# Reordering the head of a fused attention and feed-forward kernel: K/V products pair by pair, input weights in row blocks of 512 columns, hidden units in fours

## The chip, the cores and the metric

The kernel runs on one core of a Trainium2 chip. The time is the device time of one execution in microseconds (us); lower is better. Most executions of one kernel here lie within about 1 us of each other, and much of this study is about differences of 0.3 to 1.5 us in 286, so every version was timed in several rounds beside the kernel before, and each profile, which is one single execution, is used for what happens inside it and not for its total.

A ratio below is the mean time of one kernel's fast runs over that of the other's fast runs of the same rounds, so it is not quite the ratio of the medians that stand beside it.

## The reference

Eight batches of linear attention (softmax of q over the 64 features, softmax of k over the 576 rows, so that K and V shrink to a 64x64 matrix per head), followed by a feed-forward block with 2048 hidden units and a Swish with one beta per unit.

```python
q_s = softmax(q, axis=-1)                       # q, k, v: (8, 8, 576, 64) f32
k_s = softmax(k, axis=2)
kv  = einsum('bhsd,bhse->bhde', k_s, v)
x   = einsum('bhsd,bhde->bhse', q_s, kv)        # then reshaped to (4608, 512)
h   = x @ w_in                                  # (512, 2048)
g   = h * (1 / (1 + exp(-beta * h)))
out = g @ w_out                                 # (2048, 512), out f32
```

## The kernel before

TensorE multiplies in bf16. The tokens are cut in nine slabs of 512. A slab has a first phase (`pass1`: 16 tiles of 128 hidden units, each the sum of four matmuls over the input pairs m = 0 to 3) and a second phase (`pass2`: 64 matmuls into four output tiles). The K/V products and attention outputs of the next batch are woven between the matmuls of the slab before. Slab 0 has nothing before it, so its attention (the *head*) is bare, and batch 1's attention is squeezed into the end of slab 0 (the *transition*) because its data land late (a load of V for batch 1 at 40.0 us by the chain of the kernel before).

Names in the code and the profiles: EK holds the exponentials of k and VB the values in bf16, whose products are the K/V products; KVD is a K/V product after normalisation, QT the transposed softmax of q, XT the attention output, which is the input of the first phase; WIN and WOUT are the two weight matrices in bf16 (w_out divided by beta), GT the hidden units after the Swish, PS a bank of PSUM, which every matmul on the pages has as its output.

The parts that matter (cuts are marked with `...`):

```python
WCH = ((0, 256), (256, 256), (512, 512), (1024, 512), (1536, 512))   # chunks of w_in columns

def pass1_mm(t, f, m, bk):
    ...
    n = 2 if f < 8 else 4            # hidden units of tile f: every n-th column
    l = bass.AP(WIN, m * DFF + 128 * (f // n * n) + f % n, [[NM * DFF, 128], [n, 128]])
    mm(PS[bk][:, :], l, x[:, m, :], m == 0, m == NM - 1, ...)

def homes_ek(i, e_, r=()):           # zero the unused blocks of EK; r only says when
    z = EK[i][64 * e_:64 * e_ + 64, :, :, 64 * (1 - e_):64 * (2 - e_)]
    add(POOL, lambda e: e.memset(z.bitcast(F32), 0.0), r=r, w=[("ekz", i, e_)])

# head: K/V products of all pairs, then the outputs; pairs 2 and 3 in halves
kv_mm(0, 0, 3, 0); kv_mm(0, 1, 3, 1)
for hp in range(2): kvd(0, hp, 3, VW * hp)          # VectorE: normalise into KVD
kv_mm(0, 2, 5, 0, D + 1); out_now(0, 0, 4, ACTE)
kv_mm(0, 3, 5, 1, D + 1); out_now(0, 1, 6, ACTE)
...
at(0); out_halves(0, 2, 7, 3); out_halves(0, 3, 4, 5)   # only two tiles of slab 0 by m
...
for c in range(2, len(WCH)):
    for m in range(NM): cast_win(c, m, 1, DVE)      # f32 -> bf16 on VectorE
for e_ in range(2):
    homes_ek(1, e_, [("win", 3, NM - 1)])           # after the casts of columns 1024 to 1535
for c in range(3): load_wout(c)
load_main("qf", qt_h, QF, 1, 4); load_wout(3)
...
# slab 1: small products of the 64 remainder rows of batches 0 and 1
todo = spread(outr_steps(1), 101.5, 103) + attn_late(2)
```

The second number in `todo` is a position counted in matmuls of the slab: 64 is the first matmul of the second phase. QTR, which `outr_steps` reads, is filled by a transposing DMA.

The softmax here doesn't subtract the row's maximum and nothing guards it: scores larger than these inputs give would overflow.

Of the kernel before, what the change touches and what calls it, by code (L numbers as in the profile page):

```python
# [8 lines left out]
ALU = mybir.AluOpType  # L9
# [19 lines left out]
FG = {2: (0, 256, 512, 768), 4: (1024, 1536)}  # L29
WCH = ((0, 256), (256, 256), (512, 512), (1024, 512), (1536, 512))  # L30
# [128 lines left out]
def bass_efficient_attn_shen__then__act_swish_beta_kernel(  # L159
# [12 lines left out]
    with ExitStack() as es:  # L172
# [363 lines left out]
        def out_halves(b, hp, *bks):  # L536
            i = b % 2
            for e_, (eng, key, bk) in enumerate(((DVE, "xt", bks[0]), (ACTE, "xh", bks[1]))):
                c = slice(256 * e_, 256 * e_ + 256)
                mm(PS[bk][:, c], KVD[i][:, hp, :], QT[i][:, hp, c], True, True,  # L540
                   r=kvk(i, hp) + [("qt", i, hp)], w=[("ps", bk)], bk=bk)
                add(eng, lambda e, eng=eng, bk=bk, c=c: (e.copy if eng == ACTE else e.tensor_copy)(
                    XT[i][:, hp, c], PS[bk][:, c]),
                    r=[("ps", bk)], w=[(key, i, hp)], bank=[bk])

        def go(steps):
            for s in steps:
# [6 lines left out]
        SKEY = ([("wst", 0, 0), ("wst", 0, 1), ("wst", 2)], [("wst", 1), ("wst", 3)], [("o2", 1, u) for u in range(4)],  # L554
                [("o2", 0, u) for u in range(4)])

        def load_wout(c):
            n = 2 if c < 2 else 4
            a = bass.AP(wout_h, 512 * c * DM, [[n * DM, 128], [128 * n * DM, 4 // n], [1, n * DM]])
            o = bass.AP(STAGE[c], 0, [[4 * DM, 128], [n * DM, 4 // n], [1, n * DM]])  # L560
            add(SP, lambda e: e.dma_start(o, a), w=SKEY[c],  # L561
                slot=f"wst{c}")

        def scale_wout(c):
            for f in range(4 * c, 4 * c + 4):
                add(DVE, lambda e, f=f: e.tensor_scalar(
                    WOUT[:, f, :], STAGE[c][:, f % 4, :], RB[:, f:f + 1], None, ALU.mult),
                    r=SKEY[c] + ["rb"], w=[("wout", f)])


        HEAD = (1, 2, 3, 4, 5, 6, 7)

        def wkeys(c, m, nm):
            if c == 0:
                return [("wst", 0, h) for h in range(m // 2, (m + nm + 1) // 2)]
            if c == 2:
                return SKEY[1][m // 2:(m + nm + 1) // 2]
            return SKEY[0][2:] if c == 1 else SKEY[c - 1]

        def load_win(c, m=0, nm=NM):  # L580
            c0, n = WCH[c]
            a = bass.AP(win_h, m * 128 * DFF + c0, [[DFF, 128], [128 * DFF, nm], [1, n]])
            s = STAGE[c0 // 512][:, m:m + nm, c0 % 512:c0 % 512 + n]
            add(SP, lambda e: e.dma_start(s, a), w=wkeys(c, m, nm), slot=f"win{c}{m}")  # L584

        def cast_win(c, m, nm, eng):
            c0, n = WCH[c]
            x = m if nm == 1 else slice(m, m + nm)
            s = STAGE[c0 // 512][:, x, c0 % 512:c0 % 512 + n]
            add(eng, lambda e: e.tensor_copy(WIN[:, x, c0:c0 + n], s), r=wkeys(c, m, nm),  # L590
                w=[("win", c, y) for y in range(m, m + nm)])

        def turn_beta():
            bb, c0 = kb, 16
            for g, n, o in ((4, 4, 0), (2, 2, 0), (2, 2, 256)):
                for k_ in range(n):
                    mm(bass.AP(PS[bb], c0 + o // 128 + k_, [[512, 128], [4, g]]),
                       bass.AP(BT, o + k_, [[512, g], [n, 128]]), IDF[0:g, 0:g],
                       True, True, r=["bt", "idf"], w=[("ps", bb)], bk=bb, tr=True)

        def read_beta():
            bb, c0 = kb, 16
            pb = PS[bb][:, c0:c0 + NF]
            add(DVE, lambda e: e.tensor_scalar(BC[:, :], pb, -1e-20, None,
                                               ALU.is_gt),
                r=[("ps", bb)], w=["bc0"], bank=[bb])
            yield
            add(DVE, lambda e: e.scalar_tensor_tensor(BC[:, :], pb, 1e-20, BC[:, :],
                                                      ALU.is_lt, ALU.mult),
                r=[("ps", bb), "bc0"], w=["bc"], bank=[bb])  # L610
            add(DVE, lambda e: e.scalar_tensor_tensor(BETA[:, :], BC[:, :], 4e-20,
                                                      pb, ALU.mult, ALU.add),
                r=["bc", ("ps", bb)], w=["beta"], bank=[bb])
            yield
            add(DVE, lambda e: e.reciprocal(RB[:, :], BETA[:, :]), r=["beta"], w=["rb"])
            yield
# [5 lines left out]
        kb = bank(HEAD)  # L622
        warm(3, 0, True)
        exp_q(0)
        exp_kh(0, 0, 1, 0)
        exp_kh(0, 0, 1, 1)
        exp_kh(0, 1, 1, 1)
        exp_kh(0, 1, 1, 0)
# [4 lines left out]
        go(t_steps(0, (0,), HEAD))  # L633
# [4 lines left out]
        go(t_steps(0, (1,), HEAD))  # L638
        warm(1, 0, True)
        for c in range(len(WCH)):  # L640
            for m in (0, 2) if c in (0, 2) else (0,):
                load_win(c, m, 2 if c in (0, 2) else NM)
        cast_v(0, 0)
        cast_v(0, 2)
        cast_v(0, 3, POOL, 1)
        for m in range(NM):
            cast_win(0, m, 1, POOL)
        cast_win(1, 0, 2, POOL)
        go(t_steps(0, (2,), HEAD))
        warm(1, 0, True)  # L650
        cast_v(0, 1, DVE)
        go(t_steps(0, (3,), (1,)))
        ksum(0, 0, kb)
        ksum(0, 1, kb)
        ksum_inv(0, kb, 0, 2, 0, 1)
        cast_v(0, 3, ACTE, 0)
# [3 lines left out]
        def pass1_mm(t, f, m, bk):  # L660
            x = XT8 if t == 8 else XT[t % 2]
            rd = [("xt8", p_) for p_ in range(4)] if t == 8 else [("xt", t % 2, m)]
            if (t, m) in ((0, 2), (0, 3), (1, 2), (1, 3)):
                rd = rd + [("xh", t, m)]
            n = 2 if f < 8 else 4
            l = bass.AP(WIN, m * DFF + 128 * (f // n * n) + f % n, [[NM * DFF, 128], [n, 128]])
            mm(PS[bk][:, :], l, x[:, m, :], m == 0, m == NM - 1,
               r=rd + [("win", c, m) for c in range(len(WCH))
                       if WCH[c][0] <= 128 * (f // n * n) < WCH[c][0] + WCH[c][1]],
               w=[("ps", bk)], bk=bk)  # L670
# [5 lines left out]
        HFIRST = ((0, 1, 2, 4, 6, 7, 0, 1, 2, 7), (0, 2, 4, 1, 3, 6, 5, 7, 4))  # L676
# [4 lines left out]
        def first_tiles(t, n):  # L681
            bks = [hbank(t, k) for k in range(n)]

            def at(m, f0=0, f1=n):
                for f in range(f0, f1):
                    pass1_mm(t, f, m, bks[f])
            return at
# [7 lines left out]
        FIRST = (2, 5)  # L695
        TT = (107, 125)
        at = first_tiles(0, FIRST[0])
        kv_mm(0, 0, 3, 0)
        kv_mm(0, 1, 3, 1)
        for hp in range(2):  # L700
            kvd(0, hp, 3, VW * hp)
        kv_mm(0, 2, 5, 0, D + 1)
        out_now(0, 0, 4, ACTE)
        kv_mm(0, 3, 5, 1, D + 1)
        out_now(0, 1, 6, ACTE)
        ksum_inv(0, 5, 2, 2, D, VW)
        kvd(0, 2, 5, 0, 2)
        at(0)
        out_halves(0, 2, 7, 3)
        out_halves(0, 3, 4, 5)  # L710
        beta = read_beta()
        next(beta)
        next(beta)
        add(ACTE, lambda e: e.activation(DUMMY[:, 1:2], WARM[:, 0:1], ACT.Silu), r=["warm"],
            w=["dummy"])
        cast_win(1, 2, 2, DVE)
        next(beta)
        for m in range(1, NM):
            at(m)
        for c in range(2, len(WCH)):  # L720
            for m in range(NM):
                cast_win(c, m, 1, DVE)
        for e_ in range(2):
            homes_ek(1, e_, [("win", 3, NM - 1)])
        for c in range(3):
            load_wout(c)
        load_main("qf", qt_h, QF, 1, 4)
        load_wout(3)
# [18 lines left out]
        def pass2_group(t, us, bks, tick):  # L747
            if t == 0:
                order = [(f, u) for f in range(12) for u in us]
                order += [(f, u) for h in (us[0:2], us[2:4]) for f in range(12, NF) for u in h]  # L750
# [14 lines left out]
        for t in range(NSLAB):  # L765
            todo = []
            if t == 0:
                todo = [(TT[k_], lambda k_=k_: go(t_steps(1, (2 * k_, 2 * k_ + 1), (1 + k_,))))
                        for k_ in range(2)]
                todo += [(120.5, lambda: (o2_evac(0, 1, 4, ACTE), o2_evac(0, 0, 3, ACTE)))]  # L770
                todo.append((100, lambda: (exp_kh(1, 2, 2, 0), exp_kh(1, 2, 2, 1))))
                todo.append((100, lambda: (norm_main(1, 2, 1), scale_wout(3), norm_main(1, 3, 1))))
                todo += spread(kv_steps(1, (0, 1), (0,)), 119, 120)
                todo += [(124, lambda: out_now(1, 0, 7, DVE)), (126, lambda: out_now(1, 1, 1, DVE))]
# [28 lines left out]
            if t == 0:  # L803
                for c in range(3):
                    scale_wout(c)
                for cs in ((0, 1), (2, 3)):
                    load_k(1, 4, cs)
                    load_v(1, 4, cs)
# [92 lines left out]
```

## Time and profile before

| | before |
|---|---|
| median of 3 runs | 286.19 us (286.06 to 286.26) |
| span of the profiled execution | 284.5 us |
| TensorE busy | 277.2 us, 97% |
| second phase of slab 0 begins | 28.82 us |
| last TensorE record ends | 280.62 us |

From the page of the kernel before: the shares of two engines, the DMA row in 40 slices of 7.1 us (tenths busy), and the engines' shares of the chain that ended last.

```profile
PE 277.2 (97%) x1578; PEld 135.8 (48%) x1578; DVE 116.6 (41%) x216; ACT 177.0 (62%) x241; POOL 37.3 (13%) x59
...
DMA  7999999995997999217970033003500120021022
...
PE 84%; DMA 9%; SPq 4%; DVE 1%; POOL 1%; issue 1%; POOLq 0%
```

TensorE is the bound, and DMA lies just under it from 7 to 64 us, where every slice reads 9. How little TensorE waits is in the waits view of the same kernel (who waited for whom: us in total, times, longest):

```profile
PE PS L368 <- DVE XT L221: 1.5, 1, 1.5
PE PS L366 <- DVE EQ L336: 0.5, 1, 0.5
PE PS L368 <- POOL VB L353: 0.5, 1, 0.5
PE PS L368 <- DVE KVD L405: 0.5, 1, 0.5
PE PS L368 <- ACT XT L532: 0.3, 1, 0.3
```

The timeline of TensorE around slab 0 (start, length, engine, line, operation, and in brackets the idle time before it). `XT,WIN` are first-phase matmuls, `WOUT,GT` second-phase ones:

```profile
13.37 0.39 PE L368 MATMUL PS<-QT,KVD 128*128 128x512 bf16 x1 [0.52 <-DVE KVD L405]
...
14.52 0.59 PE L368 MATMUL PS<-XT,WIN 128*128 128x512 bf16 x2 [0.26 <-ACT XT L532]
14.97 0.61 PE L368 MATMUL PS<-QT,KVD 128*128 128x256 bf16 x4
15.42 13.56 PE L368 MATMUL PS<-XT,WIN 128*128 128x512 bf16 x62
```

Sixty-two matmuls in a row, one every 0.216 us. In slab 7, where nothing is woven in, the 64 of the first phase take 13.81 us, 0.2158 us each; that is the pace where nothing holds TensorE, and it is used below. From the timelines of GpSimd and VectorE of the kernel before: the two memsets of `homes_ek(1, ...)`, and the casts of the last 512 input columns.

```profile
22.17 2.16 POOL L238 MEMSET EK<- 64x1152 f32 x2 [6.35 <-DVE WIN L590]
```

```profile
24.49 1.44 DVE L590 CAST WIN<-O2S 128x512 bf16<-128x512 f32 x4 [2.44 <-DMA O2S<-in_moe_w_in_dram]
```

The memsets end at 24.33 us, and the casts begin at 24.49, when the last 1 MB of input weights has landed (24.46 us by the trace). They do not overlap.

### The profile page before, as it was taken

What the parts mean: (1) busy time and instruction counts of PE and PEld (TensorE: products, weight loads), DVE (VectorE), ACT (ScalarE), POOL (GpSimd) and SP (SyncE); (2) the same over time, 40 slices, a digit from 0 to 9 for tenths busy, and PEclk for the clock granted to TensorE, in tenths of its full rate; (3) what the DMA queues carried; (4) which work ended last, traced back from release to release, by engine and by line L of the source; (5) the groups of instructions that cost most, each with busy time, mean ns of one, the idle gap of its engine ahead of it and who ended that gap; (6) DMA issues with size and microseconds to landing.
All of it is one profiled execution on the core that took longest, in us unless ns stands there. A gap on an engine that the chain in (4) does not pass through costs nothing.

```text
span 284.5 us, 3882 instructions
## 1 busy us (share of the span) xinstructions
PE 277.2 (97%) x1578; PEld 135.8 (48%) x1578; DVE 116.6 (41%) x216; ACT 177.0 (62%) x241; POOL 37.3 (13%) x59
## 2 busy tenths in 40 slices
PE   7999999999999999999999999999999999999994
PEld 3645445445455445544454445444544444444441
DVE  4864786019881348123831473045705200110021
ACT  5788648989977926795579637892650185028400
POOL 6612031306102032200130000000000000000000
PEclk9999999999999999999999999999999999999999
DMA  7999999995997999217970033003500120021022
GB/s 246 379 385 411 384 386 377 345 379 96 294 380 185 386 323 348 59 32 257 376 92 1 2 149 73 2 1 128 114 0 0 43 107 0 0 92 58 0 74 74
DMA packets 41451, 50.07 MB, mean 176 GB/s; under 512 B 20181, under 2 KB 29397, under 8 KB 40153
## 3 DMA queue, kind: packets, MB, share of 16 engines
q1 hardware_dynamic: 40560, 48.77, 53.9%
q10 hardware_dynamic: 872, 1.06, 1.2%
q8 instruction: 12, 0.20, 0.3%
q14 instruction: 7, 0.05, 0.1%
HBM read 36.71 MB, written 9.44 MB: 162 GB/s over the span
## 4 chain that ended last, share of the span: by engine, by line
PE 84%; DMA 9%; SPq 4%; DVE 1%; POOL 1%; issue 1%; POOLq 0%
PE PS L368 83%; DMA O2S<-in_moe_w_in_dram 5%; DMA VF<-in_v_dram 4%; SPq L261 3%; SPq L584 1%; POOL VB L353 1%; DVE WIN L590 0%; SPq L251 0%; DVE O2S L731 0%; DVE KVD L405 0%; PE PS L366 0%; SPq L561 0%; DVE RC L426 0%; POOLq L142 0%
## 5 line engine op out<-in xcount | busy, mean ns | idle before, releaser
L672 ACT ACTIVATE GT<-PS,BETA 128x512 bf16<-128x512 f32 x144 | 97.3, 689 | 77.3 <-PE PS L368 77.1
L368 PE MATMUL PS<-WOUT,GT 128*128 128x512 bf16 x576 | 132.6, 379 | 0.0
L368 PE MATMUL PS<-XT,WIN 128*128 128x512 bf16 x576 | 132.0, 379 | 0.3 <-ACT XT L532 0.3
L368 PEld LDWEIGHTS PS<-XT,WIN 128*128 128x128 bf16 x576 | 60.1, 106 | 59.1 <-POOL WIN L590 0.8
L368 PEld LDWEIGHTS PS<-WOUT,GT 128*128 128x128 bf16 x576 | 54.5, 98 | 63.0 <-DVE O2S L731 0.2
L731 DVE COPY O2S<-PS 128x512 f32<-128x512 f32 x33 | 22.7, 688 | 110.5 <-PE PS L368 110.5
L368 PE MATMUL PS<-VB,EK 128*128 128x65 bf16 (+2 forms) x306 | 35.0, 191 | 0.5 <-POOL VB L353 0.5
L353 POOL CAST VB<-VF 128x576 bf16<-128x576 f32 (+1 forms) x31 | 22.3, 720 | 76.1 <-DMA VF<-in_v_dram 47.9
L309 ACT ACTIVATE EK<-KF 64x1152 bf16<-64x1152 f32 x24 | 27.8, 1157 | 0.4
L368 PEld LDWEIGHTS PS<-VB,EK 128*128 128x128 bf16 x306 | 21.6, 98 | 7.0 <-POOL VB L353 1.0
L334 DVE TENSOR_REDUCE QS<-EQ 128x8 f32<-128x512 bf16 (+1 forms) x22 | 20.1, 914 | 3.3 <-ACT EQ L297 3.1
L443 DVE CAST XT<-PS 128x512 bf16<-128x512 f32 x24 | 16.4, 690 | 10.9 <-PE PS L368 10.9
L297 ACT ACTIVATE EQ<-QF 128x512 bf16<-128x512 f32 x32 | 17.9, 619 | 2.8 <-DMA QF<-in_q_dram 2.4
L336 DVE TENSOR_TENSOR EQ<-EQ,QI 128x1024 bf16<-128x1024 bf16 (+1 forms) x16 | 17.2, 1072 | 0.5
L368 PE MATMUL PS<-QT,KVD 128*128 128x512 bf16 (+1 forms) x36 | 12.0, 356 | 0.6 <-DVE KVD L405 0.5
L319 ACT ACTIVATE EK<-KF 64x1152 bf16<-64x1152 f32 (+1 forms) x10 | 9.5, 967 | 4.4 <-DMA KF<-in_k_dram 4.1
L336 POOL TENSOR_TENSOR EQ<-EQ,QI 128x512 bf16<-128x512 bf16 x6 | 6.3, 1042 | 23.7 <-DVE QI L335 23.5
L368 PE MATMUL PS<-XT 128*128 128x512 f32 x12 | 7.9, 775 | 1.5 <-DVE XT L221 1.5
L405 DVE TENSOR_TENSOR KVD<-PS,RC 64x128 bf16<-64x128 f32 (+2 forms) x24 | 8.0, 333 | 1.2 <-PE PS L368 0.4
L342 DVE TENSOR_REDUCE QRS<-EQR 128x8 f32<-128x512 bf16 x4 | 2.7, 681 | 13.4 <-ACT EQR L324 13.4
L297 ACT ACT_TABLE_LOAD x5 | 6.4, 1283 | 0.1
L672 ACT ACT_TABLE_LOAD x5 | 6.4, 1283 | 0.1
(51 smaller groups left out, 75.7 us busy)
## 6 DMA issues: line engine op xcount, KB each, us to landing
out_dram<-O2S SPq DMA_DIRECT2D x8, 1024.0 KB, 5.5
KF<-in_k_dram SPq DMA_DIRECT2D x6, 1152.0 KB, 9.5
VF<-in_v_dram SPq DMA_DIRECT2D x6, 1152.0 KB, 12.5
QF<-in_q_dram SPq DMA_DIRECT2D x6, 1024.0 KB, 7.7
KF<-in_k_dram SPq DMA_DIRECT2D x8, 288.0 KB, 7.9
VF<-in_v_dram SPq DMA_DIRECT2D x8, 288.0 KB, 8.4
O2S<-in_moe_w_in_dram SPq DMA_DIRECT2D x2, 1024.0 KB, 12.7
WST<-in_moe_w_out_dram SPq DMA_DIRECT2D x2, 1024.0 KB, 10.5
```

What stands on the lines that cost most here:

```text
L261: add(engs[c % len(engs)], lambda e, a=a, o=o: e.dma_start(o, a), w=[(name, i, hp) for hp in range(c * n, c * n + n)], slot=f"{name}{i}_{c}")
L297: add(ACTE, lambda e, o=o, a=a: e.activation(o, a, ACT.Exp), r=[("qf", i, hp)], w=[("eq", i, hp)])
L309: add(ACTE, lambda e, o=o, a=a: e.activation(o, a, ACT.Exp), r=[("kf", i, h) for h in hps], w=[("ek", i, h, e_) for h in hps])
L319: add(ACTE, lambda e: e.activation(o, a, ACT.Exp), r=[("kf", i, h) for h in hps], w=[("ek", i, h, e_) for h in hps])
L334: add(DVE, lambda e: e.tensor_reduce(s_, a, AX.X, ALU.add), r=ks, w=[("qs", i, hp0)])
L336: add(eng, lambda e: e.tensor_tensor(a, a, vb, ALU.mult), r=ks + [("qi", i, hp0)], w=ks)
L353: add(eng, lambda e: (e.copy if eng == ACTE else e.tensor_copy)(o, a), r=[("vf", i, hp), ("vone", i)], w=[("vb", i, hp, h) for h in ((0, 1 ...
L368: add(PE, lambda e: e.matmul(o, l, r_, start=start, stop=stop), r=r, w=w, bank=[bk])
L405: add(DVE, lambda e, o=o, a=a, s_=s_: e.tensor_tensor(o, a, s_, ALU.mult), r=[("ps", bk)] + [("rc", i, h) for h in hps], w=[("kvd", i, h, ...
L443: add(eng, lambda e: (e.copy if eng == ACTE else e.tensor_copy)(XT[i][:, hp, :], PS[bk][:, :]), r=[("ps", bk)], w=[("xt", i, hp)], bank=[bk])
L672: add(ACTE, lambda e: e.activation(GT[:, f, :], PS[bk][:, :], ACT.Silu, scale=BETA[:, f:f + 1]), r=[("ps", bk), "beta"], w=[("gt", f)], ba ...
L731: add(eng, lambda e: (e.copy if eng == ACTE else e.tensor_copy)(O2S[t % 2][:, u, :], PS[bk][:, :]), r=[("ps", bk)], w=[("o2", t % 2, u)], ...
```

## The change

The intent: start slab 0 earlier, and let the DMA order follow need.

- Head: each pair's K/V product is followed by its normalisation and output, so pair 0 does not wait for pair 1; four tiles of slab 0 then go by input pair, with pairs 2 and 3 finished in between. Twelve tiles go in groups of four by m.
- Input weights come in blocks of 512 columns; the first two blocks by row block (256 KB), the last two in halves (512 KB).
- Hidden units are taken in fours for all tiles: a tile reads every fourth column.
- w_out's last 1 MB is cut in three, and batch 1's K and V go by pairs among it; more small steps at the transition.

```diff
-WCH = ((0, 256), (256, 256), (512, 512), (1024, 512), (1536, 512))
...
-            n = 2 if f < 8 else 4
-            l = bass.AP(WIN, m * DFF + 128 * (f // n * n) + f % n, [[NM * DFF, 128], [n, 128]])
+            l = bass.AP(WIN, m * DFF + 512 * (f // 4) + f % 4, [[NM * DFF, 128], [4, 128]])
...
+        for c in range(4):
+            for m in range(0, NM, 1 if c < 2 else 2):
+                load_win(c, m, 1 if c < 2 else 2)
...
-        kv_mm(0, 0, 3, 0)
-        kv_mm(0, 1, 3, 1)
-        for hp in range(2):
-            kvd(0, hp, 3, VW * hp)
...
+        kv_mm(0, 0, 7, 0)
+        kvd(0, 0, 7, 0)
+        go(t_steps(0, (3,), (6,)))
+        kv_mm(0, 1, 1, 0)
+        kvd(0, 1, 1, 0)
...
+        at = by_m(0, 0, 4)
+        at(0)
+        out_now(0, 2, 0, DVE)
+        at(1, 0, 2)
+        out_now(0, 3, 7, ACTE)
+        at(1, 2)
...
         for e_ in range(2):
-            homes_ek(1, e_, [("win", 3, NM - 1)])
-        for c in range(3):
-            load_wout(c)
-        load_main("qf", qt_h, QF, 1, 4)
-        load_wout(3)
+            homes_ek(1, e_, [("win", 2, NM - 1)])       # the same columns, 1024 to 1535
+        load_wout(0)
+        load_wout(4)
+        load_main("qf", qt_h, QF, 1, 4, (0, 1))
+        load_wout(8)
+        load_main("qf", qt_h, QF, 1, 4, (2, 3))
+        load_k(1, 4, (0, 1))
+        load_wout(12, 2)
+        load_v(1, 4, (0, 1))
+        load_wout(14, 1)
+        load_wout(15, 1)
...
```

## The prediction

> **What bounds the kernel now.** TensorE. The page has PE busy 277.2 of 284.5 us (97%) and PE at 83% of the chain that ended last. [...] The timeline has 62 input-weight matmuls in 13.56 us, so one 512-column matmul starts every 0.2155 us. The waits view gives PE only about 3.3 us of waits: 1.5 at the start, 0.5 (EQ), 0.5 (KVD) and 0.3 (XT) in the head, 0.5 at 41.8 us for VB of batch 1; then nothing until 280.6 us. Slabs 2 to 8 are untouched, so about 2 us at most can be won.
>
> A second bound lies just under PE there: the page's DMA row is at 9 tenths from 7 to 57 us, at 377 to 411 GB/s. The chain runs through it (w_in 14.4 us, V of batch 1 10.2 us). Regrouping moves no fewer bytes; it only reorders landings.
>
> **What changes.**
> - Head: beta needs 4 transposes instead of 8 (about 0.5 us less). One of the fp32 warm matmuls (1.08 us) becomes a short bf16 one (0.22). K/V products go pair by pair, each with its normalisation, so pair 0 starts at about 10.8 us. The V casts set the pace of pairs 2 and 3 (V landed near 11.4 and 12.15 us): about 12.45 and 12.85 us.
> - Slab 0: the first four tiles go by input pair: from about 13.5 us (14.52 before), with pairs 2 and 3 finished between. By my walk with trace durations (copies 0.59 on ACT and 0.69 on DVE, KVD halves about 0.3, casts 0.42) 16 tile matmuls are done at 17.4 us; before, at 15.42+14x0.2155 = 18.4. Gain about 1.0 us. The remaining 48 then run without a wait, except perhaps 0 to 0.3 us at the last 512 columns (landed 24.46 before, now wanted near 24.7, cast included). The second phase starts near 27.9 (28.82 before).
> - Transition: w_out in tiles of four with the last 1 MB cut in three, V of pairs 0 and 1 ahead of its last 0.5 MB: 0.5 MB at 0.385 MB/us is 1.3 us earlier, so about 38.7 us. PE now wants it 4 matmuls sooner (0.9 us) and on a clock 0.9 us ahead. Expect 0.2 to 0.6 us of wait at the first K/V product and 0.3 to 0.5 at the first XT of batch 1, whose DVE chain stands behind the scaling of the last two w_out tiles: 0.3 to 0.5 us more waiting than the 0.53 before. [...]
>
> All of it is on PE's path, but only 1.0 gained and 0.3 to 0.5 returned.
>
> **Prediction.** 285.5 us, 8 in 10 between 284.6 and 286.8. Faster by over 2%: 0.02; within 2%: 0.95; slower: 0.03.
>
> **Signs.** Timeline, PE: tile matmuls from 13.2 to 13.9 us, the second phase beginning between 27.6 and 28.3 us, slab 1's uninterrupted matmuls about 0.5 us sooner. Waits, PE: no more than 0.5 us for XT or WIN in slab 0; 0.5 to 1.1 us for VB, EK, KVD or QT between 37 and 48 us. After 50 us no new wait; last PE record 0.4 to 1.2 us sooner.
>
> **What would make it wrong.** An in-order engine standing on a late landing: DVE on the first weight row before pair 2's KVD, ACT on pair 2's K before it copies XT. Weight rows landing late. [...] Batch 1 landing over 1 us later.

What is cut from the record at the marks is a general remark on shares of busy time, a risk that no run shows, and one term: 0.2 us less TensorE work in the transition, from whole copies in place of halves of 256 columns. The traces don't show that term: two halves took 0.22 us before (47.56 to 47.78 us), one whole product 0.23 after (48.18 to 48.41). The sum as its last line states it is 286.2 - 1.0 + 0.3 to 0.5 = 285.5 to 285.7 us, given as 285.5; with the term it would be 285.3 to 285.5. Two statements without a number there are in the traces: both pages move 50.07 MB, and VectorE did take its work in order behind a late landing after the change: idle for 0.46 us, it cast the first weight row from 13.02 us, and inverted the sums of pair 2, whose product had ended at 12.89, only at 13.48.

## The result, and the profile after

| | before | after |
|---|---|---|
| median, 6 runs each | 286.23 us (286.06 to 287.20) | 286.36 us (285.72 to 286.63) |
| ratio of the fast runs | | 0.9996 (95%: 0.9978 to 1.0014) |
| tile matmuls of slab 0 begin | 14.52 | 13.59 |
| second phase of slab 0 begins | 28.82 | 28.80 |
| slab 1's uninterrupted matmuls begin | 48.64 | 48.41 |
| slab 2 begins | 76.34 | 76.23 |
| last TensorE record ends | 280.62 | 280.96 |

No difference that can be told from noise. The rows of the table are start times from the TensorE timelines of the two profiles, and they say where a gain came and went. TensorE's timeline of the changed kernel, as above:

```profile
13.59 1.03 PE L366 MATMUL PS<-XT,WIN 128*128 128x512 bf16 x4 [0.20 <-DVE WIN L564]
14.46 0.38 PE L366 MATMUL PS<-QT,KVD 128*128 128x512 bf16 x1
14.67 0.59 PE L366 MATMUL PS<-XT,WIN 128*128 128x512 bf16 x2
15.10 0.38 PE L366 MATMUL PS<-QT,KVD 128*128 128x512 bf16 x1
15.32 9.47 PE L366 MATMUL PS<-XT,WIN 128*128 128x512 bf16 x43
25.30 3.66 PE L366 MATMUL PS<-XT,WIN 128*128 128x512 bf16 x15 [0.51 <-DVE WIN L564]
```

Sixteen tile matmuls are issued by 15.32 + 10 x 0.2158 = 17.48 us; before it was 15.42 + 14 x 0.2158 = 18.44. The head did gain 0.96 us. Then it is lost: 43 matmuls from 15.32 should be followed by the next at 24.60, and it comes at 25.30 (0.70 us, of which the view calls 0.51 idle); the last 15 take until 28.80, 3.50 us where 15 x 0.2158 = 3.24 (0.26). Together 0.96 us. TensorE's waits after:

```profile
PE PS L366 <- DVE XT L219: 1.5, 1, 1.5
PE PS L366 <- DVE WIN L564: 0.7, 2, 0.5
PE PS L366 <- DVE KVD L403: 0.5, 1, 0.5
PE PS L366 <- ACT VB L351: 0.4, 1, 0.4
```

WIN is new. The timelines of GpSimd and VectorE there, and then the durations of those four casts (minimum, median, maximum in ns):

```profile
22.62 2.33 POOL L236 MEMSET EK<- 64x1152 f32 x2 [6.83 <-DVE WIN L564]
```

```profile
23.08 2.82 DVE L564 CAST WIN<-O2S 128x512 bf16<-128x512 f32 x4 [0.58 <-DMA O2S<-in_moe_w_in_dram]
```

```profile
L564 DVE CAST WIN<-O2S x4: 406/646/1358, 23.1 to 25.5; 128x512 bf16<-128x512 f32 x4
```

The same four casts took 1.44 us in a row before and take 2.82 now; singly they are 0.88, 1.36, 0.41 and 0.41 us. The first half of the data came earlier (cast from 23.08 and not 24.49 us, because the load was cut in two), and ran into the memsets, which had not moved out of its way. The second half landed at 24.41 us, no earlier than before. That is the first theory: GpSimd holds up VectorE.

The second loss needs the table and not the waits: from slab 2 to the end the changed kernel falls from 0.11 us ahead to 0.34 behind although no wait is listed there. The first phases of slabs 3 to 6 last 14.93, 14.94, 14.93 and 14.94 us before, and 15.01, 15.03, 15.02 and 15.03 after; slab 2's 15.05 and 15.15. The second phases agree to 0.02 us. Slab 3 as an example, its first matmuls of either phase, before and then after:

```profile
106.30 1.89 PE L368 MATMUL PS<-XT,WIN 128*128 128x512 bf16 x8
121.23 4.48 PE L368 MATMUL PS<-WOUT,GT 128*128 128x512 bf16 x20
```

```profile
106.29 1.89 PE L366 MATMUL PS<-XT,WIN 128*128 128x512 bf16 x8
121.30 4.48 PE L366 MATMUL PS<-WOUT,GT 128*128 128x512 bf16 x20
```

What differs in all slabs is the page's weight-load group (last columns: busy us, mean ns). Before, then after:

```profile
L368 PEld LDWEIGHTS PS<-XT,WIN 128*128 128x128 bf16 x576 | 60.1, 106 | 59.1 <-POOL WIN L590 0.8
```

```profile
L366 PEld LDWEIGHTS PS<-XT,WIN 128*128 128x128 bf16 x576 | 64.5, 113 | 58.0 <-DVE WIN L564 1.4
```

Before, half of the tiles read every second column (98 ns) and half every fourth (113 ns); after, all read every fourth. Second theory: the coarse stride costs where short K/V matmuls are woven in. In the first phases of slabs 7 and 8, where nothing is woven in, both kernels take 13.81 us. (Why it costs there, no run shows.)

In the transition the changed kernel is 0.21 us better (28.80 to 48.41 against 28.82 to 48.64), with a wait of 0.47 us for KVD.

### The profile page after: what moved, and what is told of

It reads as the page before. It is cut to its first block, busy times and chain, and to the rows that moved or that the text cites. A ratio compares the mean times of both kernels' runs of the same rounds, so it can differ in the third digit from the quotient of the medians.

```text
span 284.8 us, 3870 instructions
## 1 busy us (share of the span) xinstructions
PE 277.8 (98%) x1569; PEld 137.8 (48%) x1569; DVE 119.7 (42%) x219; ACT 176.3 (62%) x240; POOL 39.3 (14%) x58
## 2 busy tenths in 40 slices
DMA packets 41050, 50.07 MB, mean 176 GB/s; under 512 B 20292, under 2 KB 28484, under 8 KB 39624
## 4 chain that ended last, share of the span: by engine, by line
PE 85%; DVE 5%; DMA 4%; SPq 3%; ACT 1%; issue 0%
PE PS L366 85%; DMA O2S<-in_moe_w_in_dram 4%; DVE WOUT L553 2%; SPq L560 2%; SPq L259 1%; DVE QS L332 1%; DVE WIN L564 1%; DVE EQ L334 1%; ACT L295 0%; DVE QT L384 0%; SPq L249 0%; DVE QI L333 0%; DVE O2S L704 0%; ACT GT L637 0%; ACT EQ L295 0%
## 5 line engine op out<-in xcount | busy, mean ns | idle before, releaser
L366 PEld LDWEIGHTS PS<-XT,WIN 128*128 128x128 bf16 x576 | 64.5, 113 | 58.0 <-DVE WIN L564 1.4
L704 DVE COPY O2S<-PS 128x512 f32<-128x512 f32 x34 | 23.3, 687 | 110.5 <-PE PS L366 110.5
L366 PE MATMUL PS<-VB,EK 128*128 128x65 bf16 (+2 forms) x306 | 35.8, 192 | 0.5 <-ACT VB L351 0.4
L351 POOL CAST VB<-VF 128x576 bf16<-128x576 f32 x31 | 23.3, 753 | 74.8 <-DMA VF<-in_v_dram 49.7
L366 PEld LDWEIGHTS PS<-VB,EK 128*128 128x128 bf16 x306 | 22.6, 99 | 7.7 <-ACT VB L351 0.7
L366 PE MATMUL PS<-QT,KVD 128*128 128x512 bf16 x32 | 12.1, 380 | 0.5 <-DVE KVD L403 0.5
L317 ACT ACTIVATE EK<-KF 64x576 bf16<-64x576 f32 (+1 forms) x12 | 9.9, 839 | 3.8 <-DMA KF<-in_k_dram 3.6
L334 POOL TENSOR_TENSOR EQ<-EQ,QI 128x512 bf16<-128x512 bf16 x7 | 7.4, 1052 | 22.5 <-DVE QI L333 22.3
L403 DVE TENSOR_TENSOR KVD<-PS,RC 64x64 bf16<-64x64 f32 (+2 forms) x28 | 8.6, 308 | 1.2 <-PE PS L364 0.3
L340 DVE TENSOR_REDUCE QRS<-EQR 128x8 f32<-128x512 bf16 x4 | 2.7, 679 | 13.2 <-ACT EQR L322 13.2
```

The source lines that it names most:

```text
L317: add(ACTE, lambda e: e.activation(o, a, ACT.Exp), r=[("kf", i, h) for h in hps], w=[("ek", i, h, e_) for h in hps])
L334: add(eng, lambda e: e.tensor_tensor(a, a, vb, ALU.mult), r=ks + [("qi", i, hp0)], w=ks)
L351: add(eng, lambda e: (e.copy if eng == ACTE else e.tensor_copy)(o, a), r=[("vf", i, hp), ("vone", i)], w=[("vb", i, hp, h) for h in ((0, 1 ...
L366: add(PE, lambda e: e.matmul(o, l, r_, start=start, stop=stop), r=r, w=w, bank=[bk])
L403: add(DVE, lambda e, o=o, a=a, s_=s_: e.tensor_tensor(o, a, s_, ALU.mult), r=[("ps", bk)] + [("rc", i, h) for h in hps], w=[("kvd", i, h, ...
L704: add(eng, lambda e: (e.copy if eng == ACTE else e.tensor_copy)(O2S[t % 2][:, u, :], PS[bk][:, :]), r=[("ps", bk)], w=[("o2", t % 2, u)], ...
```

## The experiments

Twelve kernels ran. All were correct. The kernel before was timed beside them in every call (medians 286.35, 286.54 and 286.61 us over 11 runs each). The four controls ran on another chip, so kernels are best compared by their ratios to the kernel before. The table collects what is read from their profiles; times in us.

| version | second phase of slab 0 | first phases, slabs 3 to 6 | last PE record | median | ratio to before (95%) |
|---|---|---|---|---|---|
| before | 28.82 | 14.93 to 14.94 | 280.62 | 286.23 | |
| after | 28.80 | 15.01 to 15.03 | 280.96 | 286.36 | 0.9996 (0.9978 to 1.0014) |
| e1 memset early | 28.94 | 15.01 to 15.02 | 281.04 | 286.38 | 1.0000 (0.9988 to 1.0012) |
| e2 V casts on ScalarE | 28.09 | 15.01 to 15.03 | 280.21 | 286.18 | 1.0000 (0.9983 to 1.0017) |
| e3 both | 28.12 | 15.01 to 15.03 | 280.54 | 286.18 | 0.9991 (0.9979 to 1.0004) |
| e4 both, and scaling on ScalarE | 28.38 | 15.01 to 15.03 | 280.01 | 285.75 | 0.9987 (0.9973 to 1.0000) |
| s2 stride two | 28.87 | 14.91 to 14.92 | 280.47 | 285.74 | 0.9979 (0.9964 to 0.9993) |
| b4 before, more stride four | 29.02 | 14.98 to 14.99 | 280.65 | 286.77 | 1.0019 (1.0000 to 1.0039) |
| s2e4 stride two and e4 | 28.11 | 14.91 to 14.92 | 279.90 | 285.95 | 0.9982 (0.9967 to 0.9996) |
| s2e4o and remainder later | 28.24 | 14.91 to 14.92 | 279.27 | 284.92 | 0.9948 (0.9935 to 0.9961) |
| s2o without the three edits | 28.22 | (see text) | 279.77 | 285.41 | 0.9962 (0.9949 to 0.9974) |
| forced collision | 29.35 | (see text) | 280.35 | 286.01 | 0.9987 (0.9974 to 1.0000) |
| before, last load split | 28.86 | 14.93 to 14.94 | 280.48 | 286.50 | 0.9999 (0.9985 to 1.0013) |

The boundaries are starts of merged timeline rows; one boundary of slab 5 was not clean in s2o and in the forced collision (their other phases read 14.91 to 14.92).

### Four kernels around VectorE and GpSimd

**e1** moves the memsets about 4 us earlier, into a stretch that was taken to be idle on VectorE. The `r` of `homes_ek` only says when they may start; nothing else reads that EK before batch 1.

```diff
-            homes_ek(1, e_, [("win", 2, NM - 1)])
+            homes_ek(1, e_, [("win", 1, NM - 1)])
```

> The changed kernel with one dependency altered: the two GpSimd memsets of batch 1's EK blocks wait for the casts of input columns 512 to 1023 and not of 1024 to 1535, so they run near 18 to 20.5 us, where VectorE is idle. Theory A (VectorE's casts of the last 512 columns were held by those memsets): the four casts from about 23.1 us take 0.42 us each again (before this run 0.88, 1.36, 0.41, 0.41), TensorE's wait of 0.51 us near 25.3 us falls to 0.2 or less, the second phase starts at 28.0 to 28.2 us and not 28.80; of that some 0.4 us reaches the end, because the wait for KVD near 43 us grows from 0.47 to about 0.8: end time 0.3 to 0.5 us below the changed kernel. Rival B (the casts were slow because the second half of the same columns was landing in the staging buffer, or the data came late): casts stay over 0.8 us, nothing moves.

Measured: 286.38 us, no change. The memsets ran from 18.89 to 21.22 us, and the casts of the last 512 columns are short again. But VectorE was not idle there: the first two casts of columns 1024 to 1535 now fall under the memsets and take 0.53 and 1.36 us. From the timelines of GpSimd and VectorE of e1:

```profile
18.89 2.33 POOL L236 MEMSET EK<- 64x1152 f32 x2 [2.56 <-DVE WIN L564]
```

```profile
19.69 1.81 DVE L564 CAST WIN<-O2S 128x512 bf16<-128x512 f32 x2 [0.77 <-DMA O2S<-in_moe_w_in_dram]
```

```profile
22.67 0.76 DVE L564 CAST WIN<-O2S 128x512 bf16<-128x512 f32 x2 [1.16 <-DMA O2S<-in_moe_w_in_dram]
23.94 0.76 DVE L564 CAST WIN<-O2S 128x512 bf16<-128x512 f32 x2 [0.51 <-DMA O2S<-in_moe_w_in_dram]
25.29 0.76 DVE L564 CAST WIN<-O2S 128x512 bf16<-128x512 f32 x2 [0.59 <-DMA O2S<-in_moe_w_in_dram]
```

The cause of the slow casts is confirmed; the time is not. And the edit moved the collision and did not remove it: these casts have slack, since TensorE uses the second of them only at 21.66 us, 0.16 us after its end. The same holds for e3, e4, s2e4 and s2e4o (1.36 us for that cast in each). In this execution the last 512 columns landed late (casts from 23.94 and 25.29 us; in e3, which has the same loads, from 23.09 and 24.44), the head was 0.5 us late too, and TensorE waited for the landing (0.27 us idle in the view at 25.77 us; 0.6 us by start times up to the second phase). The landing times of equal loads differ between executions: the last columns by up to 0.9 us, and the second half of the block before them, which releases the memsets of the changed kernel, by 1.9 us (20.72 us in e3, 22.64 in e1). As a prediction of time this one missed.

**e2** takes the next suspect: at 34.1 and 38.6 us GpSimd multiplies and casts while VectorE scales w_out. From the changed kernel's VectorE timeline, two scalings:

```profile
38.96 1.69 DVE L553 TENSOR_SCALAR WOUT<-O2S,RB 128x512 bf16<-128x512 f32 x2
```

GpSimd casts V from 38.62 for 1.75 us. The edit moves these two casts to ScalarE, between `exp_kh(1, 0, 2, ...)` and `exp_kh(1, 2, ...)`:

```diff
                 exp_kh(1, 0, 2, 1)
+                cast_v(1, 0, ACTE)
+                cast_v(1, 1, ACTE)
...
-                for hp in range(NHP):
+                for hp in range(2, NHP):
                     cast_v(1, hp)
```

> The changed kernel with the value casts of batch 1's pairs 0 and 1 on ScalarE and not on GpSimd. Theory A (the transition is set by VectorE's chain, lengthened by sharing with GpSimd): the scaling of w_out tiles 12 and 13 takes 0.42 us each and not 0.84, the chain up to KVD is 0.8 us shorter, TensorE's wait for KVD near 43 us goes from 0.47 to about 0; end time 0.4 us below the changed kernel, slab 0 unchanged (second phase at 28.8). Rival B (the transition is set by the landing of batch 1's K and V, so by the DMA): the wait stays near 0.5 us under KVD or another name and the time does not move.

Measured in e2's profile: the same two scalings

```profile
38.49 0.87 DVE L553 TENSOR_SCALAR WOUT<-O2S,RB 128x512 bf16<-128x512 f32 x2
```

and no wait for KVD. So VectorE's chain, and not a landing, had set that wait. A surprise is the second phase at 28.09: nothing in slab 0 was edited. In this execution the third block of columns landed earlier, the memsets ran at 21.63 and had 0.70 us to go when the last columns arrived at 23.09, so one cast was held and not two (0.98 us; no WIN wait beyond 0.2). Whether the collision hurts depends on the landing times of the single execution. And yet the median is 286.18 us, a ratio of 1.0000, where 0.4 us less than the changed kernel was expected: the profile shows a new wait of 0.5 us, for QTR, near 68 us.

**e3** has both edits.

> Both edits. If the changed kernel's gain of 1.0 us in the head was lost to two collisions of VectorE with GpSimd, this keeps it: second phase at about 28.1 us, wait for KVD at most 0.4 us, slab 1's uninterrupted matmuls at 47.3 to 47.7 us (48.41 in the changed kernel, 48.64 in the kernel before), end time 0.7 to 1.1 us below the changed kernel, ratio to the kernel before 0.996 to 0.998. If DMA sets the transition, the earlier second phase only waits longer there and the time stays within 0.3 us of the changed kernel.

Measured: second phase at 28.12, slab 1's uninterrupted matmuls at 47.26 (1.15 us ahead of the changed kernel), no wait for KVD. The end is 280.54, only 0.42 us ahead, and the median is 286.18. Of the 1.15 us, 0.7 is in one line of its waits:

```profile
PE PS L366 <- DMA QTR<-EQR: 0.7, 1, 0.7
```

Slab 2 began at 75.95, 0.28 us ahead of the changed kernel. The lower bound that I had given for the gain was missed because a third wall stood behind the two.

**e4** adds the scaling of w_out tiles 14 and 15 on ScalarE.

```diff
+                for f in (14, 15):
+                    add(ACTE, lambda e, f=f: e.activation(
+                        WOUT[:, f, :], STAGE[3][:, f % 4, :], ACT.Copy, scale=RB[:, f:f + 1]), ...)
...
-                        (112.1, lambda: scale_wout(14, 2)),
```

> Both edits, and w_out tiles 14 and 15 scaled on ScalarE in the idle stretch that it has from about 40.2 to 41.4 us, which takes 0.87 us off VectorE's chain ahead of KVD. If VectorE's chain is still what sets the first attention output of batch 1, the wait for KVD vanishes and the end is a further 0.1 to 0.4 us sooner than with both edits; if it is K and V landing by now, it equals it, with the wait named VB, EK or WOUT.

Measured: 285.75 us against e3's 286.18; VectorE now idles 0.57 us for TensorE before it inverts the sums. The gain is of the size expected, but the two intervals overlap (0.9973 to 1.0000 and 0.9979 to 1.0004), so it is not shown.

### Two kernels on the stride

**s2** takes the hidden units in twos: every second column for all tiles, w_out rows and beta to match.

```diff
-            l = bass.AP(WIN, m * DFF + 512 * (f // 4) + f % 4, [[NM * DFF, 128], [4, 128]])
+            l = bass.AP(WIN, m * DFF + 128 * (f // 2 * 2) + f % 2, [[NM * DFF, 128], [2, 128]])
...
-            a = bass.AP(wout_h, (512 * c + x) * DM, [[4 * DM, 128], [1, n * DM]])
+            a = bass.AP(wout_h, (128 * (f // 2 * 2) + f % 2) * DM,
+                        [[2 * DM, 128], [256 * DM, h], [1, w * DM]])
...
-                   bass.AP(BT, k_, [[512, 4], [4, 128]]), IDF[0:4, 0:4],
+                   bass.AP(BT, 256 * (k_ // 2) + k_ % 2, [[512, 4], [2, 128]]), IDF[0:4, 0:4],
```

> The changed kernel with units of the hidden layer taken in twos (every second column of the input weights, as the kernel before has it for its first eight tiles), w_out rows and beta to match; nothing else. Seen so far: a weight load of every fourth column takes 113 ns and of every second 98, and the first phases of slabs 3 to 6, where K/V products are woven in, take 15.01 to 15.03 us in every version with fours against 14.93 in the kernel before. Theory (the coarser stride costs in the later slabs): those phases fall to 14.93 and slab 2's from 15.15 to 15.05 or less, 0.35 to 0.45 us in all, the end comes 0.3 to 0.5 us sooner than in the changed kernel; slab 0 and the transition as in the changed kernel. Rival (pace differs by the granted clock of the single execution): phases stay at 15.01 to 15.03.

Measured: phases of 14.91 to 14.92 us, slab 2's 15.02, and all 576 weight loads at 98 ns:

```profile
L366 PEld LDWEIGHTS PS<-XT,WIN 128*128 128x128 bf16 x576 | 55.7, 98 | 64.1 <-DVE WIN L566 1.1
```

In slab 3, for the comparison with the two above:

```profile
106.22 1.89 PE L366 MATMUL PS<-XT,WIN 128*128 128x512 bf16 x8
121.13 4.48 PE L366 MATMUL PS<-WOUT,GT 128*128 128x512 bf16 x20
```

Slabs 2 to 6 are 0.13 + 0.10 + 0.12 + 0.10 + 0.11 = 0.56 us shorter than in the changed kernel (from unrounded starts; slabs 3 to 6 by 0.10 to 0.12 each). The end is 0.49 us sooner in the profiles, the ratio 0.9979 (its interval overlaps that of the changed kernel, so the step between these two is shown by the phases and not by the total). This execution had the collision again (casts of 0.41 to 1.36 us, second phase at 28.87), so the two effects are separate.

**b4** is the reverse, in the kernel before: tiles 4 to 7 in fours as well.

```diff
-            n = 2 if f < 8 else 4
+            n = 2 if f < 4 else 4
```

(with w_out and beta to match)

> The reverse, in the kernel before: tiles 4 to 7 in fours as well, so three quarters of the tiles have the coarse stride and not half. The K/V products are woven into tiles 2 to 8, so about half of these places change. Theory: the first phases of slabs 3 to 6 go from 14.93 to between 14.95 and 15.00, the end is about 0.2 us later. Rival: 14.93.

Measured: phases of 14.98 to 14.99, halfway between 14.93 and 15.02, in all four slabs; 286.77 us, ratio 1.0019 (1.0000 to 1.0039). The dose fits. That the total is 0.2% longer is at the edge of the interval.

### Two kernels on the wall at 68 us

**s2e4** is e4 with the stride of two, **s2e4o** the same with the remainder products three to four matmuls later. They may not go later still: the K/V products of batch 2 overwrite the KVD that they read.

```diff
-                todo = spread(outr_steps(1), 101.5, 103) + attn_late(2)
+                todo = spread(outr_steps(1), 104.5, 105.3) + attn_late(2)
```

> The three edits of the fourth run (early memsets, value casts and the last scaling on ScalarE) with the stride of two. If head, transition and stride add up: 0.4 us below the fourth run, about 285.3 us, ratio to the kernel before 0.9965 to 0.9980, unless TensorE now waits for the transposed remainder rows (QTR) near 68 us, which seem to land at 67.6 to 68.1 us however early TensorE comes: then up to 0.7 us of it goes there.

> As the run before, with the small products of the remainder rows of batches 0 and 1 placed three to four tile matmuls later in slab 1 (among batch 2's K/V products). If the landing of the transposed rows near 68 us is the next wall, the wait for QTR is gone and the end comes up to 0.5 us sooner than in a run that shows the wait, about 285.0 us; if the rest of the way is set by something else, no difference.

The waits of s2e4 have this line, and those of s2e4o none for QTR:

```profile
PE PS L366 <- DMA QTR<-EQR: 0.8, 1, 0.8
```

Measured: s2e4 waits 0.75 us for QTR and takes 285.95 us, above the range that I gave for "adding up" and within what I gave for the wait. In s2e4o the wait is gone and the median is 284.92 us, 0.9948 of the kernel before: the fastest version, and clear of it. The step from s2e4, 1.03 us between medians, is more than the wait of 0.75 us and than the 0.63 us between the two profiles; what the rest is was not found. This is the version to keep.

Why QTR is a wall: the transposing DMA is issued at 64.8 us in the kernel before and lands 2.6 us later, near 67.4; in e3 it is issued at 63.6 and takes 4.5 us, to 68.1; in s2e4o 63.5 and 4.8. Asked 1.2 us sooner, it comes no sooner. In the five profiles that were asked (before, after, e3, s2e4, s2e4o) it landed between 67.4 and 68.3 us, whether issued at 63.4 or at 64.8. The windows view of these five has a mean DMA share of 1.04 to 1.25 from 60 to 65 us, with the loads of the coming batches. What sets its landing was not shown: no run here took the loads away, and later transposes of the kernel before took 2.6 us (issued at 86.9 and 144.2 us) and 4.0 us (203.3), so its time also varies for reasons not looked into.

### Four controls

**again** is the changed kernel unaltered, for a second profile.

> The changed kernel itself once more, for a second profile of it, since a profile is one execution and the landing times of the same transfers have differed by up to 0.9 us between profiles. Theory: first phases of slabs 3 to 6 at 15.01 to 15.03 us again (they don't depend on landings); in slab 0 one or more of the last four casts over 0.8 us wherever the memsets overlap them, and the second phase between 28.0 and 29.0 depending on it; end 285.7 to 286.7 us.

Its profile: from about 6 us on the granted clock was 0.75, 366.55 us in all, so it says nothing here. The other five runs took 285.99 to 287.74 us (ratio 1.0009).

**Forced collision**: the fastest version, with the memsets released by the first cast of the last columns.

```diff
-            homes_ek(1, e_, [("win", 1, NM - 1)])
+            homes_ek(1, e_, [("win", 3, 0)])
```

> The fastest version (stride of two, both ScalarE edits, remainder later), with the memsets now released by the first cast of the last 512 columns, so that they must overlap the second and third cast. Theory A (a GpSimd memset holds a VectorE cast for its whole length): two of those casts take 0.9 to 1.5 us and not 0.42, TensorE waits 0.4 to 0.9 us near 25 us for WIN, the second phase starts 0.5 to 0.9 us later than 28.24, and since nothing else is slack now, the end comes 0.4 to 0.9 us later than the fastest version's 284.9. Rival B (the casts were slow for another reason): 0.42 us each, 284.9 us.

From its GpSimd and VectorE timelines and TensorE's waits:

```profile
23.71 2.48 POOL L236 MEMSET EK<- 64x1152 f32 x2 [7.71 <-DVE WIN L566]
```

```profile
24.52 1.96 DVE L566 CAST WIN<-O2S 128x512 bf16<-128x512 f32 x2 [0.59 <-DMA O2S<-in_moe_w_in_dram]
```

```profile
PE PS L366 <- DVE WIN L566: 0.9, 1, 0.9
```

Two casts take 1.96 us (0.76 without the memsets), TensorE waits 0.89 us, the second phase starts at 29.35 and not 28.24, and the median is 286.01 against 284.92 us: 1.1 us, a little more than expected. The landing of the data (24.52; 24.60 in the fastest version) was the same. So a collision so placed costs about as much as the whole head had won. The ratios, which allow for the other chip, part as well: 0.9987 (0.9974 to 1.0000) against 0.9948 (0.9935 to 0.9961).

The traces also say what "holds" means. In the 13 fast profiles together 20 casts began under a memset of this kind and outlasted it, not counting one of b4 that began in its last 9 ns. Each of the 20 ended 0.28 to 0.29 us after its memset, however long it had been held (0.52 to 1.36 us from start to end, 0.41 to 0.43 when alone). So the cast stood until the memset's end, and then 0.28 us of it were left; had the two merely slowed each other, that remainder would change with the time of overlap.

**The kernel before with its last load cut in halves**, as the change has it:

```diff
-            for m in (0, 2) if c in (0, 2) else (0,):
+            for m in (0, 2) if c in (0, 2, 4) else (0,):
```

> The kernel before, with the load of its last 512 input columns cut in two halves as the change has it. Its memsets run from about 22.2 to 24.3 us; the first half now lands near 23.1 to 23.6 us, so its first two casts overlap them. Theory A: those two take 0.8 us or more; but here TensorE wants these columns only at 25.35 us and later, so it waits at most 0.3 us and the time stays within 0.3 us of before. Rival B: all casts 0.42 us.

```profile
22.58 2.33 POOL L238 MEMSET EK<- 64x1152 f32 x2 [6.33 <-DVE WIN L590]
```

```profile
23.09 2.77 DVE L590 CAST WIN<-O2S 128x512 bf16<-128x512 f32 x4 [0.63 <-DMA O2S<-in_moe_w_in_dram]
```

The collision appears in the old kernel by splitting one load alone (casts of 0.82 and 1.36 us), and costs it nothing: 0.9999. Its first 16 tile matmuls are issued only by 15.38 + 14 x 0.2158 = 18.40 us and not by 17.48, so TensorE comes 0.9 us later and has no use for the columns yet. The earlier landing brought the collision, the earlier TensorE made it cost.

**s2o** leaves out the three edits on VectorE, GpSimd and ScalarE.

> The changed kernel with only the stride of two and the remainder later: the memsets and the transition as in the change. If the three edits around VectorE and GpSimd carry the rest of the gain, TensorE still waits about 0.5 us for KVD near 43 us and, where the memsets overlap, 0.3 to 0.8 us for WIN: 285.5 to 285.9 us, like the stride alone. If they carry nothing, about 284.9 us like the fastest version.

Measured: 285.41 us, 0.9962. It waits 0.42 us for KVD, as expected, and only 0.2 us for WIN, because in its profile the memsets ran early (21.70 us). The versions with and without the three edits differ by some 0.5 us in the medians (285.41 to 284.92), but these are of different chips, and the intervals of the ratios overlap (0.9949 to 0.9974 and 0.9935 to 0.9961), so what they are worth is not shown; without the later remainder they gained nothing over the stride alone (s2e4 0.9982, s2 0.9979). The later remainder comes to about 0.3 to 0.5 us without them (s2 to s2o: 0.9979 to 0.9962, whose intervals overlap).

## Why the prediction was right or wrong, point by point

"Within 2%" and the range (284.6 to 286.8) held; the measured 286.36 is 0.86 us above the 285.5 named. That they held is partly luck: the time of the kernel before, 286.23, lies in the range too, so the range could not tell a gain from none, and the gain of 0.7 us in its middle did not come. Of the signs, the start of the tile matmuls held. Missed were the second phase (27.6 to 28.3 forecast, 28.80 measured), slab 1's matmuls (0.5 us sooner forecast, 0.23 measured), XT or WIN waits of at most 0.5 us (0.51 + 0.20) and the last record (0.4 to 1.2 us sooner forecast, 0.34 later measured); the 0.47 us for KVD lies just under its 0.5 to 1.1. Step by step:

- **TensorE bounds the kernel, DMA lies just under it, and about 2 us are to be had.** Right. The best version gained 1.5 us. (The 377 to 411 GB/s leave out a slice: from 50 to 57 us the page has 345.)
- **The head gains about 1.0 us, 16 matmuls done at 17.4.** Right: 17.48 against 18.44, 0.96 us. Tile matmuls began at 13.59 (predicted 13.2 to 13.9).
- **"The remaining 48 then run without a wait, except perhaps 0 to 0.3 us".** Wrong, and the largest miss: 0.96 us was lost there in the profile. I had costed the casts at 0.42 us each and asked only when their data land. The memsets on GpSimd, which the diff leaves in place, hold VectorE's casts: 0.88 and 1.36 us. The trace shows it: a cast that starts at 23.08 us under a memset of 22.62 to 23.67 ends at 23.96, 0.28 us after it, and the next, begun at 23.88 under the memset that lasts until 24.95, ends at 25.24. Not all of the 0.96 us is the collision's: the second half of the columns landed at 24.41 us, and in s2e4o, where no memset is near, the first 16 matmuls were issued by 17.60, that half was cast from 24.60, and TensorE lost 28.24 - 17.60 - 48 x 0.2158 = 0.28 us. By this an estimated 0.2 to 0.3 us of the loss is the late landing that the prediction allowed for, and about 0.7 the collision. The list of what would make the prediction wrong had "weight rows landing late"; it was one landing *early*. In executions where the third block lands sooner, the loss is small, so part of it is luck: with the same instructions in slab 0, the memsets ran from 21.63 us in e2, with no wait for WIN beyond 0.2, and from 22.62 in the changed kernel, with 0.51 near 25 us.
- **The transition returns 0.3 to 0.5 us.** Right in mechanism, wrong in size: the wait forecast at the first K/V product (0.2 to 0.6 us) did not appear; the KVD wait was named, and its chain behind the last w_out scalings too, but the wait is 0.47 us in place of the 0.53 before, not on top of it, and the transition as a whole was 0.21 us shorter. e2 showed that VectorE's chain sets it.
- **"Slabs 2 to 8 are untouched".** Wrong. Their instruction order is the same, but their weights are read at a stride of four columns and not two in half of the tiles. It costs about 0.09 us in each first phase with woven K/V products, 0.45 us in slabs 2 to 6 (15.15 - 15.05 = 0.10, then 0.08, 0.09, 0.09, 0.09). The waits view cannot show it: nothing waits, and each of the some 30 steps beside woven matmuls is on average 3 ns longer (0.09 us in all). s2 and b4 showed it in both directions. The diff had the line; I read it as bookkeeping.
- **After 50 us no new wait.** True of the waits, and useless, as the last point shows.

So the sum was: +0.96 head, -0.96 collision and landing, +0.21 transition, -0.12 slab 1 (48.41 to 60.19 us against 48.64 to 60.30), -0.45 stride; it gives -0.36 against the -0.34 us between the two last records. The -0.12 us of slab 1 is not the stride: these 54 matmuls take 11.78 us after and 11.76 with the stride of two, but 11.66 before and in b4, which has more of the coarse stride. The traces put it into one step: the first matmul of tile 9 starts 0.31 us after the one ahead of it and the next 0.25 later, not 0.216, and the semaphore that it waits for is that of ScalarE's activation (GT), a wait too short for TensorE's lines of the waits view (those of its weight loads have 0.4 us for GT there, and none before). By the code its PSUM bank was last used by tile 6, and by tile 0 in the kernel before; no run changed that. What stays open is how much the collision costs on average over executions, since one profile shows one draw of landing times; in the forced run it cost 1.1 us.

## What to carry to other kernels

Ask of each operand that a change re-indexes what its stride becomes in the steady part of the kernel, not only in the part that the change is about, and compare the stage lengths of two profiles: a cost of 3 ns a step has no line of its own in a list of waits. When a transfer is made to land sooner, look at what GpSimd does in the moment when VectorE casts the data (here a memset made a cast of 0.42 us last up to 1.36), and check in the trace where a memset that was moved has landed: here it fell under other casts, and only the slack of those (0.16 us in e1) made it free. And when a won microsecond does not reach the end, go on to the next wait: here three walls (a collision, a chain on VectorE, a transposing DMA) stood one behind the other, and against the kernel before the first two edits moved nothing (e1 to e3); the stride alone gave 0.2% (0.9964 to 0.9993), and 0.4% and 0.5% came only when the third wall was out of the way as well (s2o, s2e4o).
